# When the side steps of an attention loop are asked for: row maxima and logits one unit later, masks two units later, first loads four units earlier

## The chip, the core and the metric

The program runs on one core of one Trainium2 chip. The metric is the device time of one execution, in microseconds. TensorE (PE) does the matrix products and writes to PSUM; VectorE (DVE), ScalarE (ACT) and GpSimd (POOL) do the rest; SyncE (SP) issues most of the DMAs. Each engine works through its own list of instructions in order and waits on semaphores where an instruction needs another engine's result.

## What is computed

Attention over 32 heads (4 batches of 8), 768 rows and 64 columns each, in which a query sees only the keys that were assigned to the same one of 16 clusters; then a mixture of experts over the 3072 rows that come out, with a group and an expert chosen for each row.

```python
q_assign = argmax(einsum('bhsd,hcd->bhsc', q_n, c_n), -1)     # the same for k
mask = q_assign[:, :, :, None] == k_assign[:, :, None, :]
scores = where(mask, scale * (q @ k.T), -1e9)
attn = exp(scores - scores.max(-1)); attn /= attn.sum(-1) + 1e-9
x = (attn @ v), rows of all heads side by side               # 3072 x 512
# every row: group by argmax of x @ w_group, expert by argmax of x @ w_expert[g],
out = g_w * e_w * relu(x @ w1[g, e]) @ w2[g, e]
```

## The kernel before

A head has 36 blocks of 128 x 128 scores. They are worked off in **units** of 512 columns, nine to a head, so 288 units in all; `g` counts them. In unit g the program asks for, in this order: the exact scores of the unit (`fine`, L347 and L348, then the exponential on ScalarE, L352, and its low part on GpSimd, L354); one unit of rough scores (`coarse`, L305, reduced to row maxima by VectorE, L308), 18 units ahead of the exact ones; 16 products with V of the unit five back (`av`, L373 and L374); and then `beside(g)`.

`beside(g)` does the side work. Jobs are entered with `at(g, ...)` and run when unit g comes. Work that needs a buffer of the PSUM pool `psm` (two buffers) stands in the list `turns` with a due unit; at most one turn is taken in a unit, that with the lowest priority number and then the earliest due unit (`GAP = 1`). After a `yield` the rest of a generator runs one unit later. Four kinds of side work matter here:

- **Row maxima** (`rowmax(h)`): one unit after the last coarse unit of head h, VectorE reduces the maxima (L314) and ScalarE turns them to `mh` (L318). The generator then asks for a turn `RM` units later. In its turn PE transposes `mh` (L329), and ScalarE copies the result to `mr` (L332), which SP sends by DMA to one row of the head's tile `A` (L334). The first `fine` product of head h (L347) reads that row.
- **Masks** (`mask(Q)`, for the four heads 4Q to 4Q+3): six transposes of `oh` on PE (L264), an ACT pass to `mk` (L267), and eight DMAs on SP (L271 and L272). The turn was due at `pos[8]`.
- **Cluster assignment and splits** (`assign`, 36 small products at L242 and a chain on VectorE L247 to L254; `split`, `splitv` and `halves` with L181, L201, L202, L223), spread over the positions `pos[0]` to `pos[7]` of a group of four heads. `halves` takes `psm` buffers without a turn.
- **Logits** of a finished pair of heads (`logits`): `RL` units after its last `av`, SP issues a transposing DMA `xTr<-xs` (L592); three units later PE asks for a turn for 18 products (L609). The store of the same rows, `xbuf<-xs` (L577), is not tied to `RL`. After the last pair of a batch `decide` runs (the choice of experts), and after the third batch also `first`, which loads and splits the first expert's weights (L767, L787 to L795) and gathers its rows; its product `psh<-xTA` (L963) closes that chain.

The code gives an order of requests. A scheduler of the language then sets the order on each engine: an instruction may move ahead of ones that were asked for earlier, when it expects its operands and buffers to be ready first. So the order that counts is that of the built program.

Of the kernel before, what the change touches and what calls it, by code (L numbers as in the profile page):

```python
# [33 lines left out]
def attention(ctx, tc, qT, kT, vr, cen, R, DEN, cfg):  # L34
# [14 lines left out]
    WARM = 8,  # L49
    AHEAD, AHEAD0 = 18, 13  # L50
    EARLY = ()
    GAP, RM, RL = 1, 2, 8
    DVE_LO = [()] * 8
    DVE_END = (0, 2, 4, 6, 8)

# [204 lines left out]
    def mask(Q):  # L260
        oh = st["oh", Q]
        tp = ps_m.tile([P, 512], F32, name="psm").bitcast(F16)
        for c in range(NCH):
            nc.tensor.transpose(out=tp[:, c * P:(c + 1) * P], in_=oh[:, c], identity=ident)  # L264
        yield
        mk = sp.tile([P, S], F16, name="mk")
        nc.scalar.activation(out=mk, in_=tp[:, :S], func=AF.Identity, scale=mscale, bias=mbias)  # L267
        ready.add(Q)
        for i in range(4):
            h = 4 * Q + i  # L270
            nc.sync.dma_start(out=QA[h % 8][64:64 + C], in_=mk[C * i:C * i + C])  # L271
            nc.sync.dma_start(out=KA[h % 8][64:64 + C], in_=mk[64 + C * i:64 + C * i + C])  # L272
# [127 lines left out]
    def at(g, f, *a):  # L400
        jobs.setdefault(int(g), []).append((f, a))
# [24 lines left out]
    for Q in range(1, NQ):  # L426
        g0 = max(0, 9 * (4 * Q - 5) + 1)
        g1 = 9 * (4 * Q - 2) - 9 if Q > 1 else 12
        n = 9
        p0, p1 = 2 * Q, 2 * Q + 1  # L430
        pos = [int(g0 + (g1 - g0) * i / (n - 1)) for i in range(n)]
        free = max(9 * (4 * Q - 4), 0)
        if Q > 1:
            at(g0 - 4, load, p0)
            at(g0 - 4, loadv, p0)
            at(pos[0], split, p0, 0)
            at(pos[1], split, p0, 1)
        at(pos[0], load, p1)
        at(pos[0], loadv, p1)
        at(pos[2], turn, pos[2], assign(p0))  # L440
        at(max(pos[2], free), spread, p0)
        at(pos[3], split, p1, 0)
        at(pos[4], split, p1, 1)
        at(pos[5], turn, pos[5], assign(p1))
        at(max(pos[5], free), spread, p1)
        at(pos[6], splitv, p0)
        at(pos[7], splitv, p1)
        at(pos[8], turn, pos[8], mask(Q))

    def run(gen):  # L450
        for _ in gen:
# [924 lines left out]
def tile_cluster_attention_moe(ctx, tc, qT, kT, vr, cen, wr, w1, w2, out):  # L1376
# [25 lines left out]
    with ExitStack() as c:  # L1402
        attention(c, tc, qT, kT, vr, cen, R, DEN, cfg)
# [53 lines left out]
```

## Time and profile before

| | |
|---|---|
| three timed runs | 777.94, 771.64, 775.78 us; median 775.78 us |
| the profiled execution | 770.8 us, of it 768.7 us from the first to the last instruction |
| mean granted TensorE clock | 0.981 of full speed |
| busy share of the span | PE 94%, weight loads 81%, VectorE 78%, GpSimd 64%, ScalarE 58% |

Attention fills the first 414 us or so, the experts the rest. Matrix products overlap in the array and their ends are modelled, so a busy PE says little by itself; what can be read exactly is when an instruction begins and what it had waited for. In the rows further down a time is in microseconds from the start of the span, a line "start, duration, engine, line, operation, tile written <- tiles read", and a bracket at the end gives idle time of the engine and who ended it.

### The profile page before, as it was taken

What the parts mean: (1) busy time and instruction counts of PE and PEld (TensorE: products, weight loads), DVE (VectorE), ACT (ScalarE), POOL (GpSimd) and SP (SyncE); (2) the same over time, 40 slices, a digit from 0 to 9 for tenths busy, and PEclk for the clock granted to TensorE, in tenths of its full rate; (3) what the DMA queues carried; (4) which work ended last, traced back from release to release, by engine and by line L of the source; (5) the groups of instructions that cost most, each with busy time, mean ns of one, the idle gap of its engine ahead of it and who ended that gap; (6) DMA issues with size and microseconds to landing.
All of it is one profiled execution on the core that took longest, in us unless ns stands there. A gap on an engine that the chain in (4) does not pass through costs nothing. (4 is left out here: it accounts for less than half of the span.)

```text
span 768.7 us, 26315 instructions
## 1 busy us (share of the span) xinstructions
PE 724.7 (94%) x10882; PEld 619.0 (81%) x10882; DVE 598.9 (78%) x1194; ACT 444.6 (58%) x877; POOL 495.7 (64%) x522
## 2 busy tenths in 40 slices
PE   5898999999999999997898979999999999999996
PEld 3676888888888888876776857888779999999896
DVE  5997988899798988996665545868588988888761
ACT  4567867677686777755674246444534455555542
POOL 9568687889978998787852435426555555554433
PEclk9999999999999999999989979999999999999998
DMA  8759647467653765407422487866677788788721
GB/s 248 190 157 217 161 125 158 111 145 185 125 162 91 173 146 104 97 12 178 127 63 61 55 269 275 275 210 216 226 245 239 255 255 274 256 279 276 248 75 49
DMA packets 115719, 134.75 MB, mean 175 GB/s; under 512 B 34963, under 2 KB 85651, under 8 KB 115592
## 3 DMA queue, kind: packets, MB, share of 16 engines
q1 hardware_dynamic: 109820, 119.61, 56.7%
q0 software_dynamic: 5616, 13.35, 4.9%
q8 instruction: 87, 1.43, 0.8%
q14 instruction: 40, 0.33, 0.2%
q10 hardware_dynamic: 156, 0.03, 0.0%
HBM read 93.20 MB, written 14.11 MB: 140 GB/s over the span
## 5 line engine op out<-in xcount | busy, mean ns | idle before, releaser
L354 POOL TENSOR_TENSOR pl<-p 128x512 f16<-128x512 f32 x278 | 285.6, 1047 | 80.8 <-ACT p L352 75.8
L308 DVE TENSOR_REDUCE mpart<-psc 128x1 f32<-128x512 f32 (+1 forms) x282 | 190.0, 683 | 29.2 <-PE psc L305 28.5
L352 ACT ACTIVATE p<-psf 128x512 f32<-128x512 f32 x288 | 168.5, 593 | 76.5 <-PE psf L348 69.4
L373 PE MATMUL pso<-V,p 128*128 128x65 f16 x1152 | 164.0, 195 | 0.0
L373 PE MATMUL pso<-V,pl 128*128 128x65 f16 x1152 | 163.2, 195 | 0.0
L374 PE MATMUL pso<-V,p 128*128 128x64 f16 x1152 | 162.9, 192 | 0.0
L374 PE MATMUL pso<-V,pl 128*128 128x64 f16 x1152 | 162.6, 192 | 0.0
L347 PE MATMUL psf<-A 82*128 82x384 f16 (+2 forms) x576 | 145.9, 278 | 6.4 <-ACT p L352 3.8
L348 PE MATMUL psf<-B 128*128 128x384 f16 (+2 forms) x576 | 146.1, 278 | 0.0
L374 PEld LDWEIGHTS <-p 128*128 128x128 bf16 x1152 | 113.6, 99 | 21.1 <-issue 1.0
L373 PEld LDWEIGHTS <-p 128*128 128x128 bf16 x1152 | 113.2, 98 | 12.6 <-issue 4.6
L305 PE MATMUL psc<-A 80*128 80x512 f16 (+1 forms) x376 | 109.9, 334 | 5.3 <-DVE mpart L308 4.2
L374 PEld LDWEIGHTS <-pl 128*128 128x128 f16 x1152 | 113.7, 99 | 0.6 <-issue 0.2
L373 PEld LDWEIGHTS <-pl 128*128 128x128 f16 x1152 | 112.1, 97 | 0.3
L966 DVE SCALAR_TENSOR_TENSOR hl<-psh,hh 128x160 f16<-128x160 f32 (+14 forms) x136 | 50.2, 371 | 60.5 <-ACT hh L965 60.1
L965 ACT ACTIVATE hh<-psh 128x160 f16<-128x160 f32 (+14 forms) x136 | 46.5, 347 | 62.5 <-PE psh L963 62.2
L963 PE MATMUL psh<-xT,wh0a 128*128 128x288 f16 (+7 forms) x512 | 74.7, 255 | 0.0
L348 PEld LDWEIGHTS <-B 128*128 128x128 f16 x576 | 57.4, 100 | 15.8 <-issue 6.6
L925 POOL DMA_INDIRECT xg<-xbuf,ri x32 | 42.2, 1318 | 40.9 <-issue 19.8
L963 PE MATMUL psh<-xT,wh0b 128*128 128x272 f16 (+6 forms) x448 | 65.2, 254 | 1.3 <-DVE xT L937 0.7
L347 PEld LDWEIGHTS <-A 82*128 82x128 f16 x576 | 56.2, 99 | 11.5 <-DMA A<-mr 2.2
L963 PE MATMUL psh<-xT,wl0a 128*128 128x288 f16 (+7 forms) x256 | 64.0, 255 | 0.0
(303 smaller groups left out, 1688.4 us busy)
## 6 DMA issues: line engine op xcount, KB each, us to landing
st<-w SPq DMA_DIRECT2D x128, 512.0 KB
B<-parts SPq DMA_DIRECT2D x64, 192.0 KB
kx<-kT SPq DMA_DIRECT2D x16, 384.0 KB
qx<-qT SPq DMA_DIRECT2D x16, 384.0 KB
vx<-vr SPq DMA_DIRECT2D x16, 384.0 KB
A<-parts SPq DMA_DIRECT2D x32, 192.0 KB
xbuf<-xs SPq DMA_DIRECT2D x16, 384.0 KB
A<-mk SPq DMA_DIRECT2D x56, 24.0 KB
```

Of the source, the lines that this page charges most:

```text
L305: last["mm"] = nc.tensor.matmul(out=pc[:, off:off + k1 - k0], lhsT=QA[h % 8][0:80, c * P:(c + 1) * P], rhs=KA[h % 8][0:80, k0:k1], start=T ...
L308: nc.vector.tensor_reduce(out=(mp[:, 0, 0:1], mp[:, :, 1], mp[:, 1, 0:1])[i], in_=pc.rearrange("p (a x) -> p a x", a=n), axis=AX.X, op=ALU ...
L347: nc.tensor.matmul(out=o, lhsT=KA[h % 8][0:82, ks], rhs=QA[h % 8][0:82, q0:q1], start=True, stop=False)
L348: nc.tensor.matmul(out=o, lhsT=KBs[h][:, ks], rhs=QBs[h][:, q0:q1], start=False, stop=True)
L352: cfg["exp"] = nc.scalar.activation(out=p32, in_=pf, func=AF.Exp, scale=QK / (SQ * SQ))
L354: lo = (nc.vector if u in (EARLY if h < 2 else DVE_LO[h % 8] if h < NH - 2 else DVE_END) else nc.gpsimd).tensor_tensor(out=pl, in0=p32, in ...
L373: nc.tensor.matmul(out=O[:, col:col + 65], lhsT=p[:, bs], rhs=vh, start=c == 0 and q == 0 and i == 0, stop=False, skip_group_check=True)
L374: nc.tensor.matmul(out=O[:, col:col + 64], lhsT=p[:, bs], rhs=vl, start=False, stop=c == NCH - 1 and i == 1, skip_group_check=True)
L925: self.got = nc.gpsimd.indirect_dma_start(out=xg[0:n].rearrange("p k a x -> p (k a x)"), out_offset=None, in_offset=bass.IndirectOffsetOnA ...
L963: self.mm = nc.tensor.matmul(out=ph[:, 0:M], lhsT=w[:, k, fs], rhs=xT[:, a, k], start=i == 0, stop=i == 3 * KD - 1)
L965: nc.scalar.activation(out=hh[:, f], in_=ph[:, 0:M], func=AF.Relu)
L966: self.ev = nc.vector.scalar_tensor_tensor(out=hl[:, f], in0=ph[:, 0:M], scalar=0.0, in1=hh[:, f], op0=ALU.max, op1=ALU.subtract)
```

## The change

`RM` goes from 2 to 3 and `RL` from 8 to 9. The mask's turn is due two units later for all groups but the first. The first pair's loads of a group are entered at `g0 - 8` in place of `g0 - 4`.

```diff
-    GAP, RM, RL = 1, 2, 8
+    GAP, RM, RL = 1, 3, 9
+    AWAY = 2
...
         if Q > 1:
-            at(g0 - 4, load, p0)
-            at(g0 - 4, loadv, p0)
+            at(g0 - 8, load, p0)
+            at(g0 - 8, loadv, p0)
             at(pos[0], split, p0, 0)
...
-        at(pos[8], turn, pos[8], mask(Q))
+        away = AWAY if Q > 1 else 0
+        at(pos[8] + away, turn, pos[8] + away, mask(Q))
```

No instruction is added or taken away; they change places. Line numbers of the changed kernel are one or two higher (L264 becomes L265, L963 becomes L965). Three places of the built order follow, all of the group Q = 3 or of the end of attention; the tiles `A_165` to `A_172` are the eight tiles `A`, one for each head modulo 8.

First PE, the slot at the end of unit 83. Before, the row maxima of head 10 are transposed there:

```order
L374 LDWEIGHTS pl
L374 MATMUL pso<-V_173,pl 128x64
L329 LDWEIGHTS mh_205
L329 MATMUL psm<-ident,mh_205 128x128
L347 LDWEIGHTS A_166
L347 MATMUL psf<-A_166 128x384
```

In the changed kernel the same slot holds the mask's transposes (six pairs like the one shown), and the transpose for head 10 stands at the end of unit 84:

```order
L375 LDWEIGHTS pl
L375 MATMUL pso<-V_173,pl 128x64
L265 LDWEIGHTS oh
L265 MATMUL psm<-ident,oh 128x128
```

The mask moved from the middle of unit 82 to the end of unit 83, the place that the row maxima left.

Second SP, the same group, up to the row-max DMA of head 10 (tile `A_167`). Before:

```order
L577 DMA xbuf<-xs 128x6x256
L213 DMA A_165<-parts 64x2x768
L592 DMA_TRANSPOSE xTr<-xs 128x12x128
L86 DMA vx<-vr 128x768
L271 DMA A_169<-mk 16x768
L272 DMA A_169<-mk 16x768
L271 DMA A_170<-mk 16x768
L272 DMA A_170<-mk 16x768
L271 DMA A_171<-mk 16x768
L272 DMA A_171<-mk 16x768
L271 DMA A_172<-mk 16x768
L272 DMA A_172<-mk 16x768
L334 DMA A_167<-mr 1x6x128
```

In the changed kernel:

```order
L214 DMA A_165<-parts 64x2x768
L87 DMA vx<-vr 128x768
L579 DMA xbuf<-xs 128x6x256
L594 DMA_TRANSPOSE xTr<-xs 128x12x128
L272 DMA A_169<-mk 16x768
L273 DMA A_169<-mk 16x768
L272 DMA A_170<-mk 16x768
L273 DMA A_170<-mk 16x768
L272 DMA A_171<-mk 16x768
L273 DMA A_171<-mk 16x768
L272 DMA A_172<-mk 16x768
L273 DMA A_172<-mk 16x768
L335 DMA A_167<-mr 1x6x128
```

The eight mask DMAs still stand directly ahead of the row-max DMA; the store and the transposing DMA moved behind the second load of `vx`, next to the masks.

Third PE in unit 281, near the end of attention. Before, two products of the expert stage stand between the products with V:

```order
L374 MATMUL pso<-V_176,p_10642 128x64
L963 LDWEIGHTS wh_9284
L963 MATMUL psh<-xTA,wh_9284 128x288
L963 LDWEIGHTS wh_9284
L963 MATMUL psh<-xTA,wh_9284 128x288
L373 LDWEIGHTS pl
```

In the changed kernel the first of them stands behind the last product with V of all 288 units:

```order
L375 LDWEIGHTS pl
L375 MATMUL pso<-V_176,pl 128x64
L965 LDWEIGHTS wh_9320
L965 MATMUL psh<-xTA,wh_9320 128x288
```

They moved past six units of attention. The line of the diff on the loads leaves no trace in the order: a program with that line alone has the same instructions in the same order on all five engines as the kernel before.

## Rows read from the trace of the kernel before

**Rows 1.** Busy time of each engine in stretches of 50 us; then the granted clock, the busy share of the DMA engines and GB/s.

```profile
100.00:150.00 50.00, 49.55 (x976) 41.31 (x973) 43.32 (x92) 35.83 (x72) 40.29 (x40) 1.00 0.55 134
...
400.00:450.00 50.00, 41.42 (x562) 33.95 (x558) 25.41 (x77) 22.33 (x39) 14.37 (x16) 0.93 0.48 99
```

**Rows 2.** Waits of PE from 75 to 330 us: who waited for whom, us in total, times, the longest.

```profile
PE psm L264 <- DVE V L202: 1.3, 4, 0.5
PE psm L329 <- ACT mh L318: 0.3, 1, 0.3
```

**Rows 3.** The timeline around the row maxima of head 9, PE and ACT.

```profile
128.64 0.19 PE L374 MATMUL pso<-V,pl 128*128 128x64 f16 x1
128.92 0.23 PE L329 MATMUL psm<-ident,mh 128*128 128x128 f16 x1
...
128.67 0.20 ACT L318 ACTIVATE mh<-m 128x6 f16<-128x6 f32 x1
```

**Rows 4.** The timeline of the same group from the logits to the row maxima of head 10, PE, DVE and ACT.

```profile
137.02 0.61 DVE L254 TENSOR_TENSOR oh<-psm,mw 128x192 f16<-128x192 f32 x2
...
137.46 0.19 PE L374 MATMUL pso<-V,pl 128*128 128x64 f16 x1
137.69 0.37 PE L609 MATMUL psm<-WR,xTr 128*128 128x20 f16 x9
...
138.28 0.48 ACT L201 ACTIVATE psm<-vx 128x384 f32<-128x384 f32 x1
...
138.82 0.27 PE L347 MATMUL psf<-A 82*128 82x256 f16 x1
...
139.40 0.49 PE L264 MATMUL psm<-ident,oh 128*128 128x128 f16 x6 [0.32 <-DVE V L202]
...
139.94 0.99 ACT L267 ACTIVATE mk<-psm,mbias,mscale 128x768 f16<-128x768 f16 x1 [0.66 <-PE psm L264]
...
141.80 0.22 PE L329 MATMUL psm<-ident,mh 128*128 128x128 f16 x1
```

**Rows 5.** The timeline of SP's queue in that stretch.

```profile
136.20 0.38 SPq L577 DMA_DIRECT2D xbuf<-xs  x1
...
138.31 1.48 SPq L592 DMA_TRANSPOSE xTr<-xs  x1
139.89 0.87 SPq L86 DMA_DIRECT2D vx<-vr  x1
140.95 0.60 SPq L271 DMA_DIRECT2D A<-mk  x1
...
146.87 0.75 SPq L334 DMA_DIRECT2D A<-mr  x1
```

**Rows 6.** The timeline of PE, the first exact scores of heads 6, 10, 14 and 26.

```profile
103.41 0.33 PE L347 MATMUL psf<-A 82*128 82x384 f16 x1
...
149.22 0.33 PE L347 MATMUL psf<-A 82*128 82x384 f16 x1
...
195.49 0.33 PE L347 MATMUL psf<-A 82*128 82x384 f16 x1
...
333.49 0.34 PE L347 MATMUL psf<-A 82*128 82x384 f16 x1 [0.49 <-DMA A<-mr]
```

**Rows 7.** The timeline of SP's queue, the row-max DMAs of heads 6, 14 and 26.

```profile
100.41 0.76 SPq L334 DMA_DIRECT2D A<-mr  x1
...
193.21 0.75 SPq L334 DMA_DIRECT2D A<-mr  x1
...
330.48 0.74 SPq L334 DMA_DIRECT2D A<-mr  x1
```

**Rows 8.** Busy tenths of the DMA engines in 40 slices of 0.02 us, from 194.6 to 195.4 us.

```profile
DMA  0000143322100000000000000000000000000000
```

**Rows 9.** The timeline around the row maxima of head 3, ACT, SP and PE.

```profile
62.08 0.24 ACT L332 COPY mr<-psm 6x128 f16<-6x128 f16 x1
...
63.07 0.57 ACT L352 ACTIVATE p<-psf 128x512 f32<-128x512 f32 x1
...
63.96 0.83 ACT L181 ACTIVATE parts<-qx 128x768 f16<-128x768 f32 x1
...
62.35 0.85 SPq L334 DMA_DIRECT2D A<-mr  x1
...
68.06 0.34 PE L347 MATMUL psf<-A 82*128 82x384 f16 x1 [1.44 <-DMA A<-mr]
```

**Rows 10.** Busy time of the engines there and around 407 us, columns as in rows 1.

```profile
62.00:66.00 4.00, 4.00 (x69) 3.15 (x67) 3.09 (x7) 4.00 (x10) 3.48 (x4) 1.00 1.02 242
66.00:68.00 2.00, 0.62 (x17) 0.50 (x15) 2.00 (x6) 1.74 (x4) 1.56 (x3) 1.00 0.88 208
...
404.00:408.00 4.00, 1.30 (x18) 0.89 (x15) 3.32 (x7) 2.40 (x5) 1.04 (x1) 1.00 0.77 156
408.00:412.00 4.00, 4.00 (x46) 3.00 (x43) 1.18 (x2) 2.47 (x5) 1.85 (x2) 0.62 0.02 4
```

**Rows 11.** The timeline of PE at the two early products of the expert stage.

```profile
407.50 0.41 PE L963 MATMUL psh<-xTA,wh 128*128 128x288 f16 x2 [2.38 <-DMA xTA<-vx]
```

**Rows 12.** The timeline of SP's queue, store and transposing DMA of another pair.

```profile
159.70 0.39 SPq L577 DMA_DIRECT2D xbuf<-xs  x1
160.13 3.05 SPq L592 DMA_TRANSPOSE xTr<-xs  x1
```

## Prediction

> **What bounds the kernel now.** First the busy times by stretch [rows 1]: from 100 to 150 us PE is busy 49.55 of 50 us at the full granted clock, so in the steady part of attention a microsecond is won only where PE stands still. Then the waits of PE from 75 to 330 us [rows 2]: they name two pairs of lines and 1.6 us in all. That view counts only idle time by modelled ends, so I go by when instructions begin. With 976 products in 50 us they come 0.05 us apart on average [rows 1]; where the next one begins much later, PE stood. In the group of four heads around 140 us three such places stand out. The transpose of head 9's row maxima begins 0.28 us after the product ahead of it, right behind ScalarE's `mh` [rows 3]: 0.25 us lost. The logits begin 0.23 us after the product ahead, when VectorE has finished `oh` and a `psm` buffer is free [rows 4]: 0.2 us. The mask's transposes begin 0.58 us after the score product ahead, and the row itself shows 0.32 us idle behind that product's modelled end, ended by VectorE's low part of V [rows 4]: between the two I take 0.45 us. Together 0.9 us in a group; the mask lines come in six such groups (Q = 2 to 7), so 5.4 us by this one group, and less where a wait is shorter, since rows 2 list only four of the mask's. The third thing to see is off PE: SP's list. The mask's ScalarE pass ends at 140.93, the eight mask DMAs begin at 140.95, and behind them comes the row-max DMA of head 10, at 146.87 [rows 4, 5]. Head 10's first exact score, which reads it, begins at 149.22 without a wait [rows 6]. How near this is to a wait decides the case.
>
> **The change part by part.** *Loads.* The built order doesn't change by this line, as shown above, so it costs and brings nothing; what it moves in the program, the scheduler had already moved.
>
> *The three waits.* Row maxima one unit later: ScalarE has `mh` ready by then, and the assignment's products take the slot. Logits: the assignment now runs a slot earlier, so `oh` and the buffer are free before. Mask: its slot is behind unit 83, over 1 us after the low part of V. So I take all 0.9 us of a group as gone from PE's path. Nothing else is ahead of them in the rows; if they were all, the sum would be 5.4 us in six groups.
>
> *What is late next: the row maxima of heads 6, 10, ... 26.* The mask's transposes go where the row maxima of head 10 stood, at 141.80 [rows 4]. With the 0.9 us of waits and their own 0.49 us no longer ahead of that place, they begin at 141.80 - 0.9 - 0.49 = 140.41, which is 1.01 us later than before (139.40). ScalarE's pass (0.99 us) and SP's eight DMAs follow directly, as before, so the row-max DMA is issued 1.01 us later too, at 147.88. From its issue to PE's use I need a landing time. Upper bound: head 14's was issued at 193.21 and used at 195.49 with no wait, 2.28 us [rows 6, 7]. Lower bound: the DMA engines carry its packets until about 194.84 and nothing after, 1.63 us [rows 8]. I take 1.9 us, near the middle, since the semaphore still follows the data. Head 10 is then ready at 149.78; PE, 0.9 us earlier, comes at 148.32 and waits 1.46 us. The group ends 149.78 - 149.22 = 0.56 us **later** than before. In the other groups only the room differs, that is, first score minus issue: head 6 has 103.41 - 100.41 = 3.00 us, head 14 2.28, head 10 2.35 [rows 5 to 7]. With 1.01 + 1.9 - room: -0.1, +0.63, +0.56. Heads 18 and 22 I take like head 10, +0.5 each. Head 26 had 3.01 us and yet waited 0.49 [rows 6, 7], so its landing was slow; -0.1 with 1.9 us and +1.1 with what it took, so +0.5. Sum: +2.6 us. Bounds by the landing time: each group moves by 0.27 us down or 0.38 us up, so +1.0 to +4.9 us. The waits of about 1.4 us that I expect are no longer than that of 1.44 us at 68.06, whose stretch shows the full clock [rows 9, 10].
>
> The Trainium skill (DMA: Bandwidth & Descriptors, section "Rules for kernel authors") advises to issue a DMA early and to wait on its semaphore late. That speaks against asking later for steps that end in a DMA, and the room of 2.28 to 3.01 us above agrees that they are issued late already. Its section "Anatomy of one DMA — SWDGE (gpsimd) path" gives some 2.0 us of fixed cost for another path; by that figure the sum would be an estimated 0.6 us higher.
>
> *Head 3.* Its row maxima move a unit later as well, and on ScalarE a split (0.83 us) and an exponential (0.57 us) come ahead of the copy that stood at 62.08 [rows 9]. PE already waits 1.44 us for this transfer, 5.7 us after its issue, while the DMA engines are full (share 1.02, then 0.88) [rows 9, 10]. So it is bound by the transfers ahead, which don't move: between 0 and +1.4 us, and I take 0. At the upper end the wait would be near 2.8 us, and after one of 2.38 us the granted clock stood at 0.62 of full for the next 4 us, three quarters of them at 1.2 in place of 2.4 GHz [rows 10, 11]: another 1.5 us.
>
> *The end of attention.* PE waits 2.38 us for the first expert's rows at 407.50 while units of attention stand behind it in its list [rows 11]. The changed order has that product behind all products with V, so those units run through: -2.4 us, up to -3.9 us with the half clock that followed [rows 10]. The transfers themselves may come a unit later, but some 7 us of attention work now cover them. What follows attention (rows of the last pair, logits, choice of experts, table) starts from the last products with V, so this passes to the end. If ScalarE can't feed these units faster than one in 1.0 us the gain is smaller: 0 to -3.9, I take -2.4.
>
> *SP's list.* The store and the transposing DMA now stand directly ahead of the masks. The end of the transposing DMA's issue follows the store's start by 139.79 - 136.20 = 3.6 us in one pair and by 163.18 - 159.70 = 3.5 us in another [rows 5, 12]. If the store starts before 138.4 the masks don't notice; the second load of `vx` ahead of it needs ScalarE's last half of V, which ended at 138.76 [rows 4] and now stands one exponential earlier in ScalarE's list. So this is on the edge: 0 to +1.2 us in a group. I allow +0.15 us in each, +0.9 us.
>
> Sum: +2.6 + 0 - 2.4 + 0.9 = **+1.1 us**. The profiled execution took 770.8 us, 5 us under the median of the three runs, so 771.9 us by it and 776.9 us on the scale of the median, which is what I forecast: **777 us**.
>
> **The rivals.** *The waits simply go* (faster). If the row-max DMA of heads 6 to 26 is still in time, because the landing is at its lower bound or the mask's pass starts at once, the full 5.4 us come back, with 2.4 us at the end: 775.8 - 7.8 = 768 us, up to 766.5 with the clock. For it: the three waits are real. Against: the eight mask DMAs stand ahead of the row maxima in both orders, and the room of 0.4 us or so is smaller than the move of 1.01 us.
>
> *SP's list becomes the bound* (slower). If the second load of `vx` goes at 138.8 and takes 0.87 us, the store starts at 139.7, the transposing DMA is issued until 143.2, and the masks that are ready at 141.96 start 1.2 us late; as the row maxima already are the last to come, all of it counts: 6 x 1.2 = 7.2 us on top of 2.6, less 2.4 at the end, so 783 us, and 786 with head 3's. It decides from the point where the store starts after 138.4. Against: ScalarE's last half of V moved ahead.
>
> **How the numbers follow.** About 1% (7.8 us) is what a measurement of this kernel can tell from no change. The forecast, with its terms anywhere between their bounds, has 0.72; the waits simply go 0.11; SP's list 0.17. Of the first rival some half lies under 768.0, and a little of the forecast's low end: faster 0.07. Of the second, most lies over 783.5, and some of the forecast's upper end (+4.9, head 3, no gain at the end): slower 0.16. Same 0.77. The range goes from 769 us, the first rival with its waits partly gone, to 784 us, the second; the three runs shown spread by 3 to 4 us around their median, which is inside it.
>
> **What would show it.** In the changed profile PE should wait for `mr` at the first score of heads 10, 14, 18 and 22, about 1 to 1.5 us each and some 6 to 8 us in all, where before it did so once after 75 us; the waits at L329, at the logits and at the mask should be gone. The time from the first score of head 10 to that of head 14 should be 0 to 0.7 us longer than 195.49 - 149.22 = 46.27 us. The wait for `xTA` of 2.38 us should be gone and the last exponential come earlier relative to head 26. I am wrong if there is no wait for `mr` in the steady part, if it is over 2 us each with a lower clock behind it, or if attention's end shows a new wait of over 2 us.

## The result, and the profile after

The changed kernel takes 782.75 us (median of 20 runs, 772.96 to 789.43), the kernel before, timed beside it on the same chip, 772.62 us (20 runs, 766.40 to 779.58). The ratio, in which disturbed runs are left out, is **1.0085** with a 95% interval of 1.0059 to 1.0111: some 6.6 us slower, where the two medians of all runs lie 10.1 us apart. The profiled execution has a span of 775.5 us against 768.7, at a mean granted clock of 0.984 against 0.981.

First the waits of PE from 75 to 330 us, the view of [rows 2]: who waited for whom, us in total, times, the longest.

```profile
PE psf L348 <- DMA A<-mr: 5.5, 5, 1.9
PE psf L348 <- ACT p L353: 1.1, 3, 0.6
PE psm L243 <- issue: 0.6, 2, 0.5
PE psc L306 <- DVE mpart L309: 0.3, 1, 0.3
```

The waits of the mask's transposes and of the row maxima are gone, and the row-max DMA leads the list, as the prediction said. The busy time of the engines from 100 to 150 us, the stretch of [rows 1], in its columns:

```profile
100.00:150.00 50.00, 48.22 (x949) 40.27 (x946) 42.15 (x87) 35.88 (x71) 39.48 (x40) 1.00 0.58 136
```

PE did 949 products there, before 976. The first exact scores of heads 6, 10, 14, 18, 22 and 26, on the timeline of PE, answer to [rows 6]; the bracket is idle time and who ended it:

```profile
106.37 0.34 PE L348 MATMUL psf<-A 82*128 82x384 f16 x1 [1.66 <-DMA A<-mr]
...
152.75 0.34 PE L348 MATMUL psf<-A 82*128 82x384 f16 x1 [0.93 <-DMA A<-mr]
...
201.78 0.34 PE L348 MATMUL psf<-A 82*128 82x384 f16 x1 [1.86 <-DMA A<-mr]
...
247.48 0.34 PE L348 MATMUL psf<-A 82*128 82x384 f16 x1 [0.24 <-DMA A<-mr]
...
295.30 0.34 PE L348 MATMUL psf<-A 82*128 82x384 f16 x1 [0.80 <-DMA A<-mr]
...
341.85 0.34 PE L348 MATMUL psf<-A 82*128 82x384 f16 x1 [0.88 <-DMA A<-mr]
```

All six wait, 6.4 us in all; before, only head 26 did, 0.49 us. How the wait at 201.78 comes about is read from SP's queue in that group (Q = 4), and from ScalarE's mask pass and the copy that the row-max DMA sends; compare [rows 5]:

```profile
188.58 0.41 SPq L579 DMA_DIRECT2D xbuf<-xs  x1
189.15 4.87 SPq L594 DMA_TRANSPOSE xTr<-xs  x1
194.12 0.60 SPq L272 DMA_DIRECT2D A<-mk  x1
...
199.29 0.59 SPq L273 DMA_DIRECT2D A<-mk  x1
199.98 0.75 SPq L335 DMA_DIRECT2D A<-mr  x1
...
192.23 0.99 ACT L268 ACTIVATE mk<-psm,mbias,mscale 128x768 f16<-128x768 f16 x1 [0.38 <-PE psm L265]
...
193.60 0.24 ACT L333 COPY mr<-psm 6x128 f16<-6x128 f16 x1
```

The mask was ready at 193.22 and the row maxima at 193.84. SP was inside the transposing DMA until 194.02, then issued eight mask DMAs, and the row-max DMA followed at 199.98, 6.1 us after its data were there. PE began 1.80 us after that issue.

At the end of attention, [rows 11], the first product with `xTA` stands behind the last products with V and waits for nothing. But another wait remains there. VectorE stands before the ids of the first expert's rows, and the coarse scores stand behind VectorE. First VectorE and PE in the kernel before, whose rows were not read for the prediction, then the same rows after, with two windows of 4 us each from about where PE takes up again (columns as in rows 1):

```profile
382.77 0.15 DVE L849 CAST idA<-tabA 128x1 int32<-128x1 f32 x1 [4.10 <-DMA tabA<-table]
...
383.64 0.38 PE L305 MATMUL psc<-A 80*128 80x512 f16 x1 [2.45 <-DVE mpart L308]
...
384.00:388.00 4.00, 3.57 (x62) 2.89 (x59) 3.32 (x10) 1.47 (x3) 2.04 (x2) 0.63 0.00 0
388.00:392.00 4.00, 4.00 (x48) 3.14 (x47) 1.55 (x3) 1.40 (x3) 1.04 (x1) 0.52 0.01 4
```

```profile
391.81 0.15 DVE L851 CAST idA<-tabA 128x1 int32<-128x1 f32 x1 [4.18 <-DMA tabA<-table]
...
393.83 0.58 PE L306 MATMUL psc<-A 80*128 80x256 f16 x2 [3.77 <-DVE mpart L309]
...
392.00:396.00 4.00, 2.17 (x23) 1.69 (x23) 3.22 (x11) 1.47 (x3) 1.72 (x2) 0.52 0.01 1
396.00:400.00 4.00, 4.00 (x71) 3.33 (x70) 1.66 (x4) 1.47 (x4) 1.36 (x2) 0.63 0.01 4
```

Where the 6.8 us of the span went, by the first exponentials of heads 6 and 26 on ScalarE (104.17 and 334.21 before, 107.09 and 342.56 after) and the last exponential (414.13 and 418.98): +2.9 us up to head 6, +5.4 from head 6 to head 26, -3.5 from there to the last exponential, and +2.0 behind attention.

### The profile page after: what moved, and what is told of

Its sections match the earlier page's. It is cut to its first block, busy times and chain, and to the rows that moved or that the text cites. A ratio compares the mean times of both kernels' runs of the same rounds, so it can differ in the third digit from the quotient of the medians.

```text
span 775.5 us, 26322 instructions
## 1 busy us (share of the span) xinstructions
PE 724.9 (93%) x10882; PEld 618.2 (80%) x10882; DVE 602.5 (78%) x1194; ACT 443.3 (57%) x877; POOL 496.4 (64%) x522
## 5 line engine op out<-in xcount | busy, mean ns | idle before, releaser
L965 PE MATMUL psh<-xT,wh0a 128*128 128x288 f16 (+7 forms) x512 | 74.7, 255 | 0.0
L965 PE MATMUL psh<-xT,wh0b 128*128 128x272 f16 (+6 forms) x448 | 65.2, 254 | 2.1 <-DVE xT L939 1.1
L965 PE MATMUL psh<-xT,wl0a 128*128 128x288 f16 (+7 forms) x256 | 64.0, 255 | 0.0
```

Of the source, the lines that this page charges most:

```text
L965: self.mm = nc.tensor.matmul(out=ph[:, 0:M], lhsT=w[:, k, fs], rhs=xT[:, a, k], start=i == 0, stop=i == 3 * KD - 1)
```

## The experiments

All figures by stage are of one profiled execution each. "6 to 26" is the time between the first exponentials of these heads, "26 to last" that from head 26's to the last exponential of attention, "mr" the idle time of PE ended by the row-max DMA at the first exact scores of heads 6, 10, 14, 18, 22 and 26.

| kernel | ratio to before, 95% interval | 6 to 26 | mr | 26 to last |
|---|---|---|---|---|
| before | 1 | 230.0 | 0.5 | 79.9 |
| changed | 1.0085 (1.0059 to 1.0111) | 235.5 | 6.4 | 76.4 |
| e1, masks alone | 1.0028 (1.0000 to 1.0057) | 231.1 | 0 | 80.3 |
| e2, row maxima alone | 1.0110 (1.0065 to 1.0156) | 238.2 | 8.6 | 75.2 |
| e3, logits alone | 0.9908 (0.9878 to 0.9938) | 233.4 | 0.2 | 70.0 |
| e4, changed, DMA past six masks | 0.9972 (0.9945 to 0.9999) | 231.0 | 0 | 74.2 |
| e5, logits from head 25 | 0.9946 (0.9919 to 0.9973) | 231.7 | 0.9 | 75.2 |
| e6, e2 with masks put off | 1.0074 (1.0048 to 1.0101) | 238.5 | 9.0 | 75.4 |
| e7, changed, masks at old place | 1.0059 (1.0032 to 1.0086) | 237.3 | 6.9 | 77.0 |
| e8, changed, logits at old place | 1.0081 (1.0051 to 1.0111) | 242.7 | 9.3 | 72.5 |
| e9, logits from head 23 | 0.9839 (0.9798 to 0.9880) | 230.9 | 0.3 | 66.4 |
| e10, logits of head 23 only | 0.9864 (0.9827 to 0.9901) | 231.1 | 0.6 | 69.2 |
| e11, e9 with masks put off | 0.9872 (0.9834 to 0.9909) | 230.2 | 0 | 67.7 |
| e12, changed, first expert later | 1.0050 (1.0023 to 1.0078) | 235.9 | 6.1 | 68.9 |

The end of attention can be accounted for by two things. When PE's idle times (each stop of over 0.15 us) and the time lost to a lower granted clock are taken off "26 to last", 60.3 to 62.5 us are left in all fourteen profiles. These two sum to 18.6 us before (11.8 idle, 6.8 by the clock), 15.5 in the changed kernel, 8.9 in e3, 4.8 in e9, 7.4 in e10 and 5.7 in e11.

The changed kernel's ratio comes from one chip run, e1 to e4, e5 to e8, e9 to e11 and e12 from four others, each against the kernel before beside it.

**e1.** The masks alone.

```diff
-        at(pos[8], turn, pos[8], mask(Q))
+        at(pos[8] + 2 * (Q > 1), turn, pos[8] + 2 * (Q > 1), mask(Q))
```

> The kernel before with the masks' turn two units later alone. In its built order the row-max DMA of heads 6, 10, ... 26 now stands ahead of the eight mask DMAs in SP's list, not behind them. Theory 1 (the changed kernel loses because that DMA is late behind the masks): no wait for mr at these six first scores, the mask's wait on the low part of V (0.45 us in each of six groups) gone, the wait for xTA near 407 us stays: 1 to 3 us faster than before, ratio 0.996 to 0.999. Theory 2 (the loss comes from the row maxima and the assignment that change places on VectorE and ScalarE): the same as before, ratio 0.999 to 1.001. A late mask, two units nearer to the group that uses it, would show as a wait for mk's rows at heads 8, 12, ... of 1 us or more and a ratio above 1.003.

Measured: 1.0028, and no wait for `mr`, as the two trade places on SP. The wait at the mask is gone, but PE now waits for VectorE's reduction of the coarse scores behind the place that the mask left (at 95.00 us in the first group, where the mask itself now comes at 97.69), 2.2 us in five waits. So this part brings no gain, and at most 0.6% of loss; theory 1 was wrong on the gain. No wait for the masks at heads 8, 12, ... appeared.

**e2.** The row maxima alone.

```diff
-    GAP, RM, RL = 1, 2, 8
+    GAP, RM, RL = 1, 3, 8
```

> The kernel before with the row maxima's turn one unit later alone. Its built order has the masks at their old unit 82, the row maxima of the last head of a group at unit 84, the assignment's products split over two slots, and the row-max DMA behind the eight mask DMAs as before; the xTA product stands behind the last products with V. Theory 1 (what counts is where the masks stand, since the row-max DMA waits for them on SP): masks as early as before, so no or small waits for mr, under 0.5 us each; with the end of attention 2 to 4 us earlier the kernel is 1 to 4 us faster than before, ratio 0.995 to 0.999. Theory 2 (the row maxima's own later place is the loss): waits at heads 6, 10, ... 26 or on VectorE's assignment of 1 us or more a group, 4 to 8 us in all, ratio 1.003 to 1.009.

Measured: 1.0110, with an interval that overlaps that of the whole change, and theory 1 as written fell: masks "as early as before" on PE did not make them early on SP. The queue in the group Q = 6, with ScalarE's mask pass and PE's wait:

```profile
287.55 0.99 ACT L267 ACTIVATE mk<-psm,mbias,mscale 128x768 f16<-128x768 f16 x1 [0.40 <-PE psm L264]
...
286.43 4.10 SPq L592 DMA_TRANSPOSE xTr<-xs  x1
290.63 0.60 SPq L271 DMA_DIRECT2D A<-mk  x1
...
297.23 0.75 SPq L334 DMA_DIRECT2D A<-mr  x1
...
299.06 0.34 PE L347 MATMUL psf<-A 82*128 82x384 f16 x1 [2.16 <-DMA A<-mr]
```

The mask was ready at 288.54, but SP was in the transposing DMA until 290.53. In the six groups the first mask DMA starts 2.7, 1.5, 2.1, 1.5, 2.1 and 0 us after the mask pass ends; in the kernel before 0.3 at most. Theory 2's waits came, 8.6 us where it had 4 to 8, but by SP's list, not by VectorE. The turn of the row maxima pushes the assignment a slot forward and the store and transposing DMA behind the second load of `vx`, directly ahead of the masks.

**e3.** The logits alone.

```diff
-    GAP, RM, RL = 1, 2, 8
+    GAP, RM, RL = 1, 2, 9
```

> The kernel before with the logits' turn one unit later alone. Theory 1: nothing in the steady part but the logits' wait of 0.2 us a group (1 us in all); at the end the xTA product stands behind the last products with V, so the wait of 2.4 us is gone: 1 to 4 us faster, ratio 0.995 to 0.999. Theory 2 (the logits' later place pushes the choice of experts and what stands behind it at the end of attention): the expert part begins 1 to 3 us later, ratio 1.001 to 1.004.

Measured: 0.9908, 7 us faster, more than theory 1 gave. The steady part is 3.4 us longer, not 1 us shorter; the end is 9.9 us shorter, not 2.4. That asked for another cause at the end, which e5 and e9 to e12 look for. The gain in this trace is not that the wait at the ids went. VectorE still stands there; ScalarE waits behind VectorE for a row maximum, and PE behind ScalarE for an exponential:

```profile
385.33 0.15 DVE L849 CAST idA<-tabA 128x1 int32<-128x1 f32 x1 [2.26 <-DMA tabA<-table]
...
388.35 0.21 ACT L318 ACTIVATE mh<-m 128x6 f16<-128x6 f32 x1 [3.92 <-DVE m L314]
...
389.09 0.27 PE L347 MATMUL psf<-A 82*128 82x128 f16 x1 [2.34 <-ACT p L352]
...
388.00:392.00 4.00, 2.91 (x30) 2.22 (x30) 1.85 (x5) 2.04 (x5) 1.06 (x1) 0.57 0.00 0
```

**e4.** The changed kernel, with six of the eight mask DMAs of a group behind the row-max DMA.

```diff
         ready.add(Q)
         for i in range(4):
+            if i == 1 and Q > 1:
+                for _ in range(3):
+                    yield
             h = 4 * Q + i
```

> The changed kernel with one thing undone by another way: six of the eight mask DMAs of a group are issued three units later, so that SP has two ahead of the row-max DMA, not eight. All products, masks and row maxima keep the places that the changed kernel gives them. Theory 1 (the row-max DMA is late behind eight mask DMAs, 7.3 us at six heads): the row-max DMA is issued 3 to 4 us earlier, the waits for mr at heads 6, 10, ... 26 are gone, and the kernel is 5 to 8 us faster than the changed one, ratio to the kernel before 0.997 to 1.001. Theory 2 (the loss comes from the new order on VectorE and ScalarE): the mr waits go but other waits take their place, ratio 1.005 to 1.010.

Measured: 0.9972, theory 1: 8.7 us less than the changed kernel, by the two ratios. In its trace head 26 begins 6.0 us earlier than in the changed kernel, close to the 6.4 us of waits that are gone. SP's queue in the group Q = 4, and the first exact score of head 14:

```profile
187.37 3.57 SPq L595 DMA_TRANSPOSE xTr<-xs  x1
191.47 0.92 SPq L274 DMA_DIRECT2D A<-mk  x1
192.44 0.58 SPq L275 DMA_DIRECT2D A<-mk  x1
193.12 0.75 SPq L337 DMA_DIRECT2D A<-mr  x1
...
197.67 0.32 PE L350 MATMUL psf<-A 82*128 82x384 f16 x1
```

The DMA goes out two masks after the first, 4.5 us before PE needs it. GpSimd's list is the same as in the changed kernel, and the other engines' differ by a few places next to each other. So the loss of the steady part is the row-max DMA behind eight masks on SP. The view of [rows 2] of this kernel shows the second half of the story:

```profile
PE psf L350 <- ACT p L355: 3.5, 6, 1.2
PE psm L242 <- issue: 0.3, 1, 0.3
```

All three waits that the prediction counted and all waits for `mr` are gone, and yet 6 to 26 takes 231.0 us against 230.0: waits for the exponentials stand there now.

**e5.** The logits, from head 25 on.

```diff
-                at(g + RL, go, g + RL, itertools.chain(*gens))
+                late = RL + (h >= 25)
+                at(g + late, go, g + late, itertools.chain(*gens))
```

> The kernel before with the logits' turn one unit later for the last four pairs of heads alone (from head 25 on). Theory A (what the logits' turn brings, it brings at the end of attention, and in the steady part it costs): head 24 begins within 1 us of the kernel before, where the logits alone had it 5.0 us later; from the first exponential of head 26 to the last one 68 to 73 us against 79.9 us before: ratio 0.983 to 0.990, 6 to 13 us faster than before. Theory B (the gain of the logits alone hangs on all pairs): the end as before, 78 to 80 us, ratio 0.997 to 1.002.

Measured: 0.9946, between the two; the end takes 75.2 us, about half of the 9.9 us gained by the logits alone. PE still waits 2.4 us for `xTA` and 2.4 us for the coarse scores' reduction, so the later pairs don't move these two.

**e6.** The row maxima alone with e4's edit.

```diff
-    GAP, RM, RL = 1, 2, 8
+    GAP, RM, RL = 1, 3, 8
...
+            if i == 1 and Q > 1:
+                for _ in range(3):
+                    yield
```

> The row maxima's turn alone, with six of the eight mask DMAs of a group issued three units later, so that two stand ahead of the row-max DMA on SP. The transposing DMA still stands directly ahead of the masks. Theory A (in the row maxima alone all that is lost is the row-max DMA behind late masks, 11 us with the clock that fell after two of the waits): no wait for mr at heads 6 to 26 above 0.3 us, ratio 0.995 to 1.000. Theory B (the assignment and the row maxima in their new places cost on VectorE and ScalarE by themselves): the mr waits go, but 4 us or more stay, ratio 1.003 to 1.008.

The edit did not do what it was made for: in the built order all eight masks still stand ahead of the row-max DMA, and that order is e2's on all five engines. The trace agrees (first mask at 195.42 us, the row-max DMA at 201.39, Q = 4), with 9.0 us of waits where e2 had 8.6. So it tells nothing of the two theories, but shows e2's loss a second time, at 1.0074; the two ratios of this one order differ by 0.4%, and their intervals overlap.

**e7.** The changed kernel with the masks at their old place.

```diff
-        at(pos[8] + away, turn, pos[8] + away, mask(Q))
+        at(pos[8], turn, pos[8], mask(Q))
```

> The changed kernel with the masks' turn at its old place. Theory A (the masks' DMAs begin when SP has issued the transposing DMA, and the two units on the masks are hidden behind that): mr waits like those of the changed kernel or longer, 6 to 11 us at six heads, ratio 1.004 to 1.012. Theory B (as the prediction had it: the mask's transposes, 1 us later than before, push the row-max DMA): the waits shrink by about 1 us each, to under 2 us in all, ratio 0.997 to 1.002.

Here and in e8 the loads keep their old place too, which leaves the order as it is. Measured: 1.0059 and 6.9 us of waits, theory A. (One of them, 1.19 us at head 14, has no releaser in the trace; it ends 1.83 us after the row-max DMA's issue and is counted with the others.) The two units on the masks cost the changed kernel nothing that can be seen, because without them the masks wait on SP instead: in this run the first mask DMA starts 2.5, 1.6, 1.6, 1.4, 1.5 and 0 us after the mask pass ends.

**e8.** The changed kernel with `RL` at 8.

```diff
-    GAP, RM, RL = 1, 3, 9
+    GAP, RM, RL = 1, 3, 8
```

> The changed kernel with the logits' turn at its old place. Theory A (the end of attention is helped by any of the two turns, row maxima or logits, since either puts the xTA product behind the last products with V): the end of attention as in the changed kernel within 1.5 us, ratio 1.006 to 1.011. Theory B (the logits' gain of 8 us stands by itself and adds up with the others): 6 us or more slower than the changed kernel, ratio 1.015 to 1.020.

Measured: 1.0081, the same as the whole change, so the logits' gain does not add up with the row maxima's turn, theory A by the ratio. The end was 72.5 us, 3.9 less than in the changed kernel and so outside of theory A's 1.5 us, while the steady part was 7.2 us longer (PE ran at a lower clock behind two of its six waits). Beside the row maxima, the logits' turn brings nothing that these intervals of 0.3% to either side can tell.

**e9.** The logits from head 23 on.

```diff
-                at(g + RL, go, g + RL, itertools.chain(*gens))
+                late = RL + (h >= 23)
+                at(g + late, go, g + late, itertools.chain(*gens))
```

> The kernel before with the logits' turn one unit later for the pairs of heads 22-23 to 30-31 alone. The pair of head 23 ends the third batch, and behind its logits the first expert's rows are asked for, so this pair moves the xTA product behind the last products with V, as the logits alone did; with the last four pairs only (from head 25) it stayed ahead and PE waited 2.6 us. Theory A (the gain at the end is this product's place): head 22 begins within 1 us of the kernel before, from the first exponential of head 26 to the last one 69 to 72 us (79.9 before, 70.0 with the logits alone, 75.2 from head 25): ratio 0.984 to 0.991. Theory B (the gain of the logits alone at the end comes from what is moved before head 22): 75 us as from head 25, ratio 0.993 to 0.998.

Measured: 0.9839, at the edge of theory A's range; 66.4 us at the end, less than it gave. Head 22 began 3.6 us later than before, not within 1 us, though PE's order up to there is that of the kernel before (see the last section). It has the lowest ratio of all kernels here, 12 us under the one before by the medians; the intervals of e10 and e11 overlap its own.

**e10.** The logits of the pair 22-23 only.

```diff
-                late = RL + (h >= 23)
+                late = RL + (h == 23)
```

> The kernel before with the logits' turn one unit later for the pair of heads 22-23 alone: it moves the xTA product behind the last products with V and leaves the turns of the four later pairs. Theory A (the place of the xTA product is all that counts there): 2.4 us of wait gone with some of the half clock that followed it, 75 to 77.5 us from head 26 to the last exponential, ratio 0.994 to 0.998. Theory B (it takes the logits of the last pairs as well, since their wait for xTr and the coarse scores' wait for VectorE are the larger part): no more than the 2.4 us here, and the sum of both parts only in the run from head 23 on. A ratio below 0.990 would say that the later pairs do not matter.

Measured: 0.9864, so the later pairs add little to this one, and both theories gave too small a gain. One pair of the sixteen, one unit later, gives 10.7 us at the end. SP's DMA of the table's rows, the first ids on VectorE, and the 4 us windows from 380 us on:

```profile
379.60 1.30 SPq L844 DMA_DIRECT2D tabA<-table  x2
...
381.33 0.15 DVE L850 CAST idA<-tabA 128x1 int32<-128x1 f32 x1
...
380.00:384.00 4.00, 4.00 (x95) 3.52 (x92) 3.00 (x12) 1.80 (x4) 4.00 (x5) 1.00 0.05 3
384.00:388.00 4.00, 3.68 (x79) 3.22 (x76) 1.96 (x4) 2.93 (x7) 1.96 (x3) 1.00 0.02 4
```

In VectorE's built order the first ids stand behind 280 of the 282 coarse reductions, where it was 277 before (278 in the changed kernel). Counted from head 26's first exponential (334.84 us here), VectorE ends the work ahead of the ids at 46.5 us, before at 44.5, and the table's DMA is issued at 44.8 us, before at 46.6 (380.84 us). The two moves of 2.0 and 1.9 us take away nearly all of the wait of 4.10; why the DMA is earlier is not shown. The three further reductions alone don't do it: e3 and e11 have the ids behind 280 reductions too, and VectorE stands there 2.26 and 1.79 us, PE behind it 2.34 and 1.98 us. By rows: PE's wait of 2.45 us gone; the granted clock of 0.63 and 0.52 in 8 us gone, which is 4.00 x 0.37 + 4.00 x 0.48 = 3.4 us; `xTA`'s 2.38 us gone; and 4.00 x 0.38 = 1.5 us of low clock behind it [rows 10, 11]. Sum 9.8 of the 10.7 us. But these four are not all that changed. Before, PE stopped at two more places, with a low clock behind the second:

```profile
353.26 0.22 PE L347 MATMUL psf<-A 82*128 82x128 f16 x1 [1.54 <-ACT p L352]
...
360.02 0.61 PE L609 MATMUL psm<-WR,xTr 128*128 128x20 f16 x18 [2.61 <-DMA xTr<-xs]
...
360.00:364.00 4.00, 3.98 (x57) 3.10 (x58) 2.31 (x5) 2.13 (x5) 1.20 (x2) 0.64 0.01 4
```

In e10 one stop with a low clock behind it stands there, at the first score of head 28:

```profile
359.51 0.34 PE L347 MATMUL psf<-A 82*128 82x384 f16 x1 [1.56 <-DMA A<-mr]
...
360.00:364.00 4.00, 4.00 (x47) 3.19 (x45) 2.77 (x4) 2.27 (x5) 2.59 (x3) 0.57 0.05 13
```

Over the whole stretch PE's idle time went from 11.8 to 5.7 us and the loss by the clock from 6.8 to 1.7, 11.2 us for the 10.7 measured. How much of the timed gain the wait at the ids is worth isn't shown apart from the rest.

**e11.** e9 with e4's edit.

```diff
+            if i == 1 and Q > 1:
+                for _ in range(3):
+                    yield
```

> The kernel before with the logits' turn one unit later from head 23 on, and with six of the eight mask DMAs of a group issued three units later. Theory A (the row-max DMA was late in the kernel before only at head 26): 0.5 to 1 us less than the run from head 23 on, ratio equal to its own within 0.002. Theory B (masks that come later make the coarse scores of heads 8, 12, ... wait): 1 to 3 us more than that run.

Measured: 0.9872. Its order differs from e9's on SP alone. Head 26's wait for `mr` is gone, but the interval reaches from 0.9834 to 0.9909, and against e9's 0.9839 nothing can be told.

**e12.** The changed kernel, with the list of the first expert started three units later.

```diff
-... then=(lambda: go(now[0], cfg["first"]())) ...
+... then=(lambda: at(now[0] + 3, go, now[0] + 3, cfg["first"]())) ...
```

> The changed kernel with one further edit: the list of the first expert (its weights, the table's rows, the ids read from them, the gathered rows) starts three units later; row maxima, logits and masks keep the changed kernel's turns. Theory A (the changed kernel keeps at the end what the logits alone take away: VectorE stands 4.2 us before the first ids, in front of the coarse score's reductions, PE waits 3.9 us for these at 393.83 us and runs 6.8 us at the half clock): both gone, 5 to 8 us less than the changed kernel, first exponential of head 26 to the last one 69 to 72 us against 76.4; ratio 0.998 to 1.003, since the steady part's loss of 8 us stays. Theory B (the first expert's rows then come too late): PE waits 2 us or more for xTA behind the last products with V or at the first expert, ratio as the changed kernel's, 1.006 to 1.011.

Measured: 1.0050, between the theories. In the trace theory A holds: 68.9 us at the end, 7.5 less than in the changed kernel. Theory B's wait came as well, shorter. VectorE at the ids and PE at the first expert:

```profile
388.98 0.15 DVE L849 CAST idA<-tabA 128x1 int32<-128x1 f32 x1 [0.65 <-DMA tabA<-table]
...
409.37 0.30 PE L963 MATMUL psh<-xTA,wh 128*128 128x288 f16 x1 [1.70 <-DMA xTA<-vx]
```

The timed gain over the changed kernel, 0.35% or 2.7 us, is smaller than what the one trace shows, and the two intervals overlap. That the ids' wait costs the changed kernel about 7 us in every execution is therefore not shown.

## Why the prediction was right or wrong

The time of 782.75 us lies in the range of 769 to 784, and the kernel became slower, as the forecast leaned. The size was too small: +1.1 us was forecast, about 6.6 came, and two terms were wrong.

*The loads.* No run took this line apart; its order is the same, and the prediction's 0 stands as argued.

*The three waits.* They are gone, but "I take all 0.9 us of a group as gone from PE's path. Nothing else is ahead of them" **failed**. This is the first step that was mis-sized: of the 5.4 us in six groups, 4.5 are credited to the five from head 6 to head 26, and nothing came back there. e4 has none of these waits and none for `mr`, and its steady part is no shorter than before (231.0 against 230.0 us); e1 has neither the mask's wait nor one for `mr`, and takes 231.1. Where a wait left, PE came earlier to the next input: exponentials (3.5 us in e4) or reductions of the coarse scores (2.2 us in e1).

*What is late next.* The mechanism was right: the waits stand at the heads named, 6.4 us idle in all against "6 to 8", and e4 takes them away with the time. Single waits spread more than was said, from 0.24 to 1.86 us where 1 to 1.5 was expected, and head 6, with 3.00 us of room, waits 1.66. The landing was 1.80 to 1.83 us at five heads and 2.45 at head 26; 1.9 was taken. But the DMA of head 10 moved further than the 1.01 us worked out: 4.08 us later (150.95 against 146.87) where head 9's first exponential was 2.46 us later, so 1.62 us. And with the credit of 0.9 us gone, a wait is a loss in full: from head 6 to 26 it cost 5.4 us where the prediction's terms for these five heads give +2.7 and 0.75 for SP. The interval from head 10 to head 14 is 201.78 - 152.75 = 49.03 us, 2.76 longer, not 0 to 0.7.

*Head 3.* Right: its row-max DMA went out 2.7 us later (65.08 against 62.35), and yet its first score no longer waits for `mr`, only 0.40 us for ScalarE's V, and the head's first exponential is 0.4 us later than before, behind a start that is 1.0 us later at head 2.

*SP's list.* 0.9 us taken; the masks began 0.51 us after their pass in group 2, 0.90 in group 4 and 0.03 in the others, 1.5 us. The rival "SP's list becomes the bound" is the better account of the row maxima's turn by itself (e2, e7): up to 2.7 us a group, more than the 1.2 us that it was given. In the whole change the two units on the masks cover most of it, so the masks are late for one reason or the other. The Trainium skill (DMA: Bandwidth & Descriptors, section "Issuing engines are not separate DMA queues") says that starting DMAs from several engines saves only the sequencer's time to start them, usually small beside the transfer. Here that time is what counts (e4): eight masks take SP 5.0 to 5.9 us, and the row-max DMA behind them lands 1.8 us after its issue.

*The end of attention.* `xTA`'s wait is gone, and -3.5 us lies within 0 to -3.9, but that is in part luck. The sum had this one wait; the stretch holds more, and what shrank and what grew beside it nearly cancel: the first wait for `xTr` went from 2.61 to 1.11 us and one of 1.54 us for an exponential is gone, while PE waits longer for reductions of the coarse scores. What **failed** is what was left out: the wait of 2.45 us with 3.4 us of low clock behind it at 383.64 us stood in the trace before and was not read. The changed kernel keeps it, at 3.77 us, although a new wait of over 2 us there was named as a sign of being wrong. The traces of e9 and e10 are without it, those of e3 and e11 have it in another form (2.34 and 1.98 us for an exponential), and beside the row maxima's turn it stays (3.77 us in the changed kernel, 2.94 in e7, 3.78 in e8). The four kernels that move head 23's logits and no row maxima (e3, e9, e10, e11) also lack the waits of 2.61 us for `xTr` and 2.38 us for `xTA` [rows 11], so what each of the three is worth in the timed runs is not shown.

*Behind attention* the changed kernel's profile is 2.0 us longer, where the sum had nothing; over all kernels this part runs from 350.8 to 356.9 us, and no run looked for a cause, so it stays open.

## What to carry to other kernels

Before counting a wait as gain, look for what the waiting engine needs next: three waits of 0.9 us a group went and nothing came back. When a step ends in a small DMA, its place in the issuing engine's list counts more than its place on the engine that makes the data: two masks ahead instead of eight were worth 1.1%. And read every stop of PE in a stretch, with the clock behind it, before counting one of them: at the end of attention these two tell the length to within about 2 us in all fourteen profiles. Moving one pair's logits by one unit took most of them away and made this kernel 1.4% faster; one was an engine that stood in order before a slow input, with others' work behind it.

## What the runs showed of the hardware

The transposing DMA reads the same tile `xs` as the store. In the rows shown it keeps SP for 1.5 us when another DMA stands between the two [rows 5], and for 3.05 us [rows 12] to 4.87 us (above) when it follows the store directly; SP is free 3.5 to 5.4 us after the store began. Over all pairs up to 345 us in all kernels, direct followers took from 1.48 to 5.50 us. The built program has no wait of the transposing DMA for the store, so what holds SP longer isn't shown; all that is queued behind on SP waits with it (e2).

A short stop of PE doesn't always cost clock. Head 6's wait of 1.66 us in the changed kernel left the clock at full, and one of 1.61 us at the same place in e12 was followed by a low one. First the changed kernel, then e12, 4 us each:

```profile
105.90:109.90 4.00, 3.53 (x63) 2.92 (x64) 1.35 (x2) 1.79 (x3) 2.14 (x3) 1.00 0.23 54
```

```profile
105.90:109.90 4.00, 4.00 (x47) 3.05 (x45) 1.38 (x2) 1.28 (x3) 2.79 (x3) 0.57 0.05 13
```

A clock of 0.57 for 4 us is 1.7 us, as much as the wait. What decides between the two isn't shown.

Executions of one order differ by several us in a stage: before, e5, e9 and e10 have the same list on PE up to about head 26, and head 26 begins at 334.2, 334.1, 337.7 and 334.8 us. From head 6 to head 26 the four differ less, by 1.7 us (230.0 to 231.7). So a shift of 3 us in one trace is no evidence by itself; the waits with their releasers and the timed ratios are.
